# Weight conversions of the first layer in pinned slots, h·cos(h) read from PSUM, and w_in and w_out in tiles of their own

## The chip, the cores and the metric

The kernel runs on one core of one Trainium2 chip. The metric is the time of one launch in microseconds (us) of device time. Three runs of the kernel before gave 2143.59, 2143.5 and 2141.09 us, a median of 2143.5 us.

## The reference

Three layers follow one another, all in float32. Only the middle one and its inputs are touched by the change.

```python
attn_out = _attn_ref(q, k, v, w_phi)            # linear attention, 4 batches, 8 heads, 576 x 64
x = attn_out.transpose(0, 2, 1, 3).reshape(2304, 512)
h = x @ w_in                                    # 512 -> 2048
g = h * np.cos(h)
x = g @ w_out                                   # 2048 -> 512
P = sinkhorn(exp(x @ w_gate))                   # 8 rounds over 2304 x 8
out = sum_e P[:, e:e+1] * (np.maximum(x @ w1[e], 0) @ w2[e])    # 8 experts, 512 -> 1024 -> 512
```

w_in and w_out come as float64 and are used in float32.

## The kernel before, in words

Every float32 product is done as three passes: each operand is split into a high part (rounded to the matmul's format) and a low part (the remainder), and high·high, high·low and low·high are summed in PSUM (TensorE's output memory, eight banks).

**Conversion of the weights.** The chip reads the float64 words of w_in and w_out as pairs of 32-bit integers. Each of the 16 units of the middle layer (128 of its 2048 columns) has two halves, w_in and w_out, so there are 32 halves of 128x512 numbers; half h belongs to unit h // 2. A half goes through seven small steps (lines 125 to 162): `conv_fetch` loads the raw words (`raw`, two buffers), `conv_low` (ScalarE, output `csgn`), `conv_size` (VectorE, output `cmag`), `conv_floor` (VectorE, in the attention part GpSimd), `conv_high` (VectorE, a shift on `cmag` and then an operation with two inputs on `csgn`), `conv_join` (GpSimd, adds the two), `conv_round` (ScalarE, the high part in `csp`) and `conv_rest` (GpSimd, the low part; then a DMA stores both parts in the DRAM tile `wd`). The two parts are loaded back from `wd` whenever a unit is needed.

**Attention** (line 377) runs over 16 pairs of heads in a software pipeline with an order written out by hand (`ORDER`, line 534). While it runs, `pinned[0]` is true: every instruction that is issued through the wrappers `pe`, `ve`, `se` and `ge` (TensorE, VectorE, ScalarE, GpSimd; line 60) keeps its place in program order on its engine. Otherwise a planner orders the instructions of each engine by its own cost estimates. The DMAs on the SyncE queue (SP) are always placed by the planner, and each queue runs in order. Attention also converts halves 0 to 16, and half 17 up to `conv_join`.

**The middle layer** (`moe1_steps`, line 546) runs over blocks of tokens: blocks 0, 1 and 2 of 512 tokens each, then block 3 (512) together with block 4 (256). For each of the 16 units f it does `moe1_l1` (12 matmuls of 128x512 into one of two PSUM buffers `ph`, then the element-wise chain), and `moe1_l2` of unit f - 2 (12 matmuls that add into four PSUM banks `acc`). The generator stops after six matmuls of l1, at the end of l1, and twice in l2, so there are four steps per unit in the middle of a block and 64 in a block, and one more after it. After each step `tick()` issues work that was deferred, and for block 0 a piece of the conversion may follow.

The element-wise chain of a unit is: `y` (ScalarE, from `ph`), `h` (ScalarE, a copy of `ph`), `t` (ScalarE, rounds y), `y` (VectorE, t and y), then `second`: the sine (ScalarE) and h = sine times h (VectorE), and one step later `third`: `hh`, the high part (ScalarE), and `hl`, the low part (VectorE). A `ph` buffer is free again when `y` and `h` have been read out of it.

In block 0 the generator `convert` (line 356) is advanced on every second step, in three pieces per half: fetch, low, size, floor and high; join; round and rest. Where a unit is wanted before its halves are done, `next_unit` (line 540) advances `convert` until they are. `load_unit1` (line 96) loads both halves of a unit into one tile `wsp` (four buffers), in the program's order right before l1 of that unit.

After each block, `moe1_out` copies `acc` out, and `gate` (line 516) takes one `ph` buffer in the same rotation, between l1 of the next block's units 0 and 1, for the logits (`graw`, then `pick` and the copy into `logit`). The last layer follows; it does not change.

Of the kernel before, what the change touches and what calls it, by code (L numbers as in the profile page):

```python
# [9 lines left out]
F32 = mybir.dt.float32  # L10
F32R = mybir.dt.float32r
# [3 lines left out]
ALU = mybir.AluOpType  # L15
# [10 lines left out]
def kernel(ctx: ExitStack, tc: tile.TileContext, q, k, qk_rem, v, w_phi,  # L26
                         moe_w, moe2_w_gate, moe2_w1, moe2_w2, out):
    nc = tc.nc
    P = 128
    B, NP, _, MAIN = q.shape  # L30
    D = v.shape[-1]
    NTT, _, DM = out.shape
    NT = NTT * P
    NE, NQ = moe2_w1.shape[:2]
    KC = DM // P
    NF1 = moe_w.shape[0]
# [21 lines left out]
    pinned = [False]  # L58
# [16 lines left out]
    pe, ve, se, ge = Engine(nc.tensor), Engine(nc.vector), Engine(nc.scalar), Engine(nc.gpsimd)  # L75
# [17 lines left out]
    ps_h = ctx.enter_context(tc.tile_pool(name="ps_h", bufs=1, space=PSUM))  # L93
    wpool = mctx.enter_context(tc.tile_pool(name="wpool", bufs=4, side="right"))

    def load_unit1(f):
        w = wpool.tile([P, 2, 2, DM], F32R, name="wsp")
        for i in range(2):
            nc.sync.dma_start(out=w[:, i, :, :].bitcast(F32), in_=wd[f][:, i, :, :])
        return (tuple(w[:, 0, s, :].rearrange("p (k f) -> p k f", k=KC) for s in range(2)),  # L100
                tuple(w[:, 1, s, :] for s in range(2)))

    def mm3(ps, pairs):
        ops = []
# [17 lines left out]
    NHALF = 2 * NF1  # L122
    halves = {}

    def conv_fetch(h):
        raw = vpool.tile([P, DM, 2], I32, name="raw64")
        nc.sync.dma_start(out=raw.rearrange("p f t -> p (f t)"), in_=moe_w32[h // 2, h % 2])
        halves[h] = {"raw": raw}

    def conv_low(h):  # L130
        st = halves[h]
        st["sgn"] = vpool.tile([P, DM], I32, name="csgn")
        se.activation(out=st["sgn"].bitcast(F32), in_=st["raw"][:, :, 0].bitcast(U32), func=AF.Copy,
                      scale=2.0 ** -51, bias=2.0)

    def conv_size(h):
        st = halves[h]
        st["mag"] = vpool.tile([P, DM], I32, name="cmag", bufs=3)
        ve.tensor_scalar(out=st["mag"], in0=st["raw"][:, :, 1], scalar1=2 ** 31 - 1, scalar2=None, op0=ALU.bitwise_and)

    def conv_floor(h, eng):
        mag = halves[h]["mag"].bitcast(F32)
        eng.tensor_scalar(out=mag, in0=mag, scalar1=2.0 ** -15, scalar2=None, op0=ALU.max)

    def conv_high(h):
        st = halves[h]
        ve.tensor_scalar(out=st["mag"], in0=st["mag"], scalar1=3, scalar2=None, op0=ALU.logical_shift_left)
        ve.scalar_tensor_tensor(out=st["sgn"], in0=st["raw"][:, :, 1], scalar=-2 ** 31, in1=st["sgn"], op0=ALU.bitwise_and, op1=ALU.bitwise_or)

    def conv_join(h):  # L150
        st = halves[h]
        ge.tensor_tensor(out=st["mag"], in0=st["mag"], in1=st["sgn"], op=ALU.add)

    def conv_round(h):
        st = halves[h]
        st["sp"] = vpool.tile([P, 2, DM], F32R, name="csp")
        act_hi(st["sp"][:, 0, :], st["mag"].bitcast(F32))

    def conv_rest(h):
        st = halves.pop(h)  # L160
        pool_lo(st["sp"][:, 1, :], st["mag"].bitcast(F32), st["sp"][:, 0, :])
        nc.sync.dma_start(out=wd[h // 2][:, h % 2, :, :], in_=st["sp"].bitcast(F32))
# [191 lines left out]
            dve_lo(lo, raw, hi)  # L354

    def convert():
        h = B * NP + 1
        conv_round(h)
        yield
        conv_rest(h)  # L360
        done_conv[0] = (h + 1) // 2
        for h in range(h + 1, NHALF):
            if h + 1 < NHALF and h + 1 not in halves:
                conv_fetch(h + 1)
            conv_low(h)
            conv_size(h)
            conv_floor(h, ve)
            conv_high(h)
            yield
            conv_join(h)  # L370
            yield
            conv_round(h)
            conv_rest(h)
            done_conv[0] = (h + 1) // 2
            yield

    def attention():
        n = B * NP
        sts = {0: first}
        conv_fetch(0)  # L380
        conv_fetch(1)
        for i in range(n + 2):
            cur, prev, last = sts.get(i), sts.get(i - 1), sts.pop(i - 2, None)
            if i + 1 < n:
                sts[i + 1] = load_heads(*divmod(i + 1, NP))
            if cur is None and prev is not None:
                prev["pr_psum"] = {"small": ps_r.tile([P, MAIN], F32, name="sm")}
            small = cur or (prev or {}).get("pr_psum")
            for step in ORDER.split():
                if step in CONV:  # L390
                    h = i - (step in ("csp", "q"))
                    if 0 <= h < NHALF:
                        CONV[step](h)
                        if step == "c" and h + 2 < NHALF:
                            conv_fetch(h + 2)
                    continue
                if step == "KS" and cur and not prev:
                    load_values(cur)
                if step in STEP0:
                    if cur:  # L400
                        STEP0[step](cur)
                elif step in STEP1:
                    if prev:
                        STEP1[step](prev, small) if step == "Fr" else STEP1[step](prev)
                    if step == "KS" and cur:
                        load_values(cur)
                elif last:
                    {"X": lambda st: turn_x(st, small), "xh": x_high, "xl": x_low}[step](last)
# [16 lines left out]
    def moe1_l1(blk, unit, res):  # L425
        n = BW[blk]
        xh, xl = xblk[blk]
        wh, wl = unit[0]
        ph = hpsum()
        ops = []  # L430
        for c in range(KC):
            ops += [(wh[:, c, :], xh[:, c, :]), (wh[:, c, :], xl[:, c, :]), (wl[:, c, :], xh[:, c, :])]
        for i, (w, x) in enumerate(ops):
            pe.matmul(ph[:, 0:n], w, x, start=(i == 0), stop=(i == len(ops) - 1))
            if i == 5:
                yield 1.3
        h = mpool.tile([P, 512], F32, name="h", bufs=3)
        t = mpool.tile([P, 512], F32, name="t")
        y = mpool.tile([P, 512], F32, name="y")
        pool = hpool if n == MAIN else tpool[0]  # L440
        gh = pool.tile([P, n], F32R, name="hh")
        gl = pool.tile([P, n], F32R, name="hl")
        res += [gh, gl]
        se.activation(out=y[:, 0:n], in_=ph[:, 0:n], func=AF.Copy, scale=INV2PI, bias=0.25)
        se.copy(out=h[:, 0:n], in_=ph[:, 0:n])
        se.activation(out=t[:, 0:n], in_=y[:, 0:n], func=AF.Copy, bias=MAGIC)
        ve.scalar_tensor_tensor(out=y[:, 0:n], in0=t[:, 0:n], scalar=MAGIC, in1=y[:, 0:n],
                                       op0=ALU.subtract, op1=ALU.subtract)

        def second():  # L450
            se.activation(out=y[:, 0:n], in_=y[:, 0:n], func=AF.Sin, scale=-TWOPI)
            ve.tensor_tensor(out=h[:, 0:n], in0=y[:, 0:n], in1=h[:, 0:n], op=ALU.mult)

        def third():
            act_hi(gh, h[:, 0:n])
            dve_lo(gl, h[:, 0:n], gh)

        defer(MD, second)
        defer(2 * MD, third)
        yield 1.3  # L460
# [74 lines left out]
    MD = 1  # L535
    GD = 3

    units = []

    def next_unit():  # L540
        while done_conv[0] <= len(units) and done_conv[0] < NF1:
            next(conv, None)
        units.append(load_unit1(len(units) % NF1))
        return units[-1]

    def moe1_steps(*blks):
        pend = []
        for f in range(NF1 + LAG):
            if f < NF1:
                unit = next_unit()  # L550
                gs = []
                for blk in blks:
                    g = []
                    yield from moe1_l1(blk, unit, g)
                    gs.append(g)
                pend.append((f, unit, gs))
            if f >= LAG:
                f2, unit2, gs = pend.pop(0)
                for blk, g in reversed(list(zip(blks, gs))):
                    yield from moe1_l2(blk, f2, unit2, *g)  # L560
        for blk in reversed(blks):
            defer(1 if blk == B else GD, lambda blk=blk, x2=moe1_out(blk): gate(blk, *x2))
            yield 0.2
# [7 lines left out]

    pinned[0] = True
    attention()
    pinned[0] = False
    actx.close()
    hpool = mctx.enter_context(tc.tile_pool(name="hpool", bufs=4, side="right"))
    mpool = mctx.enter_context(tc.tile_pool(name="mpool", bufs=2, side="right"))
# [5 lines left out]
    for blk in range(B - 1):  # L583
        for i, _ in enumerate(moe1_steps(blk)):
            tick()
            if blk == 0 and i % 2:
                next(conv, None)
    ectx.close()

    xctx = ExitStack()  # L590
# [323 lines left out]
```

## Time and profile before

| | us |
|---|---|
| median of three runs | 2143.5 |
| the profiled execution's own time | 2141.93 |
| its span, first to last instruction | 2140.1 |
| TensorE busy in the span | 2089.5 |
| VectorE / GpSimd / ScalarE busy | 1274.5 / 1104.3 / 934.0 |

The profile's page gives the busy time of each engine, then the span in 40 slices of 53.5 us. TensorE's digits are these; slices 4 to 6 hold block 0 of the middle layer:

```profile
PE   8997989999999999999999999999999999999999
...
PEclk9999999999999999999999999999999999999999
```

A digit of 9 is a busy share of 90% or more; PEclk is the granted clock of TensorE in tenths of full speed. Busy time of TensorE counts pipelined matmuls, so the number of matmuls in a stretch says more than the share.

### The profile page before, as it was taken

What the parts mean: (1) busy time and instruction counts of PE and PEld (TensorE: products, weight loads), DVE (VectorE), ACT (ScalarE), POOL (GpSimd) and SP (SyncE); (2) the same over time, 40 slices, a digit from 0 to 9 for tenths busy, and PEclk for the clock granted to TensorE, in tenths of its full rate; (3) what the DMA queues carried; (4) which work ended last, traced back from release to release, by engine and by line L of the source; (5) the groups of instructions that cost most, each with busy time, mean ns of one, the idle gap of its engine ahead of it and who ended that gap; (6) DMA issues with size and microseconds to landing.
All of it is one profiled execution on the core that took longest, in us unless ns stands there. A gap on an engine that the chain in (4) does not pass through costs nothing.

```text
span 2140.1 us, 35117 instructions
## 1 busy us (share of the span) xinstructions
PE 2089.5 (98%) x14039; PEld 1846.2 (86%) x14039; DVE 1274.5 (60%) x2311; ACT 934.0 (44%) x1452; POOL 1104.3 (52%) x729
## 2 busy tenths in 40 slices
PE   8997989999999999999999999999999999999999
PEld 7896768878877898989999998989999998989998
DVE  6887643445448756665666655555555555555555
ACT  5675545556553334343433433343333334333431
POOL 3345310000036666765776676567667656766762
PEclk9999999999999999999999999999999999999999
DMA  7866765664330122222222211621111111111101
GB/s 237 254 181 203 279 218 196 203 231 141 125 117 30 49 80 67 90 78 67 83 74 84 62 49 50 219 70 40 50 40 50 47 43 50 40 50 40 50 30 45
DMA packets 97314, 220.01 MB, mean 103 GB/s; under 512 B 31872, under 2 KB 42368, under 8 KB 97152
## 3 DMA queue, kind: packets, MB, share of 16 engines
q1 hardware_dynamic: 97152, 217.78, 31.6%
q8 instruction: 110, 1.80, 0.4%
q14 instruction: 52, 0.43, 0.1%
HBM read 183.27 MB, written 34.47 MB: 102 GB/s over the span
## 4 chain that ended last, share of the span: by engine, by line
PE 89%; DVE 3%; issue 3%; POOL 2%; ACT 1%; DMA 1%; SPq 0%; POOLq 0%; DVEq 0%
PE py L68 36%; PE pm L68 32%; PE ph L68 8%; PE acc L68 7%; PE pk L68 2%; PE pp L68 1%; PE pn L68 1%; POOL cmag L68 1%; PE sm L68 1%; PE pu L68 1%; POOL csp L68 1%; PE px L68 0%; ACT csp L68 0%; DVE logit L818 0%; DVE r L748 0%
## 5 line engine op out<-in xcount | busy, mean ns | idle before, releaser
L794 DVE SCALAR_TENSOR_TENSOR acc<-py,logit,acc 128x512 f32<-128x512 f32 x531 | 396.6, 750 | 322.0 <-PE py L68 322.0
L68 PE MATMUL pm<-xch,w1h 128*128 128x288 f32 x1792 | 531.0, 296 | 2.8 <-DVE t L816 1.3
L68 PE MATMUL pm<-xch,w1l 128*128 128x288 f32 x1792 | 530.7, 297 | 0.0
L68 PE MATMUL pm<-xcl,w1h 128*128 128x288 f32 x1792 | 523.0, 292 | 0.0
L690 POOL TENSOR_TENSOR w1l<-raw,w1h 128x256 fp32r<-128x256 f32 x126 | 97.1, 792 | 759.9 <-ACT w1h L687 759.9
L68 PE MATMUL py<-w2h,hl 128*128 128x512 f32 x1152 | 451.6, 392 | 3.8 <-POOL hl L68 3.8
L68 PE MATMUL py<-w2l,hh 128*128 128x512 f32 x1152 | 451.2, 392 | 0.0
L68 PE MATMUL py<-w2h,hh 128*128 128x512 f32 x1152 | 450.4, 391 | 0.8 <-DVE acc L794 0.8
L68 POOL TENSOR_TENSOR hl<-r,hh 128x1152 fp32r<-128x1152 f32 x128 | 344.7, 2693 | 78.7 <-ACT hh L68 72.9
L68 PEld LDWEIGHTS pm<-xcl,w1h 128*128 128x128 f32 x1792 | 341.1, 190 | 5.2 <-issue 0.4
L68 PEld LDWEIGHTS pm<-xch,w1h 128*128 128x128 f32 x1792 | 336.6, 188 | 9.4 <-DVE t L816 1.6
L68 PEld LDWEIGHTS pm<-xch,w1l 128*128 128x128 f32 x1792 | 336.2, 188 | 0.0
L768 ACT ACTIVATE r<-r 128x1152 f32<-128x1152 f32 x128 | 149.1, 1165 | 268.5 <-DVE r L748 262.2
L68 PEld LDWEIGHTS py<-w2h,hl 128*128 128x128 f32 x1152 | 216.5, 188 | 50.3 <-POOL hl L68 4.6
L68 PEld LDWEIGHTS py<-w2h,hh 128*128 128x128 f32 x1152 | 216.7, 188 | 44.8 <-DVE acc L794 2.8
L68 PEld LDWEIGHTS py<-w2l,hh 128*128 128x128 f32 x1152 | 216.8, 188 | 42.5
L744 ACT COPY keep<-pm 128x288 f32<-128x288 f32 x256 | 102.0, 399 | 343.6 <-PE pm L68 343.5
L748 DVE TENSOR_TENSOR r<-r,pm 128x288 f32<-128x288 f32 x512 | 216.0, 453 | 41.5 <-PE pm L68 41.3
L690 POOL TENSOR_TENSOR w1l<-ssum,w1h 128x1280 fp32r<-128x1280 f32 x63 | 186.7, 2964 | 2.0 <-ACT w1h L687 0.3
L68 PE MATMUL ph<-xh,wsp 128*128 128x512 f32 x512 | 174.7, 403 | 11.0 <-DMA wsp<-wd 5.8
L748 DVE TENSOR_TENSOR r<-keep,pm 128x288 f32<-128x288 f32 x128 | 58.2, 455 | 208.1 <-PE pm L68 207.6
L68 PE MATMUL acc<-hh,wsp 128*128 128x512 f32 x512 | 169.6, 396 | 10.3 <-ACT hh L68 10.3
(143 smaller groups left out, 2849.6 us busy)
## 6 DMA issues: line engine op xcount, KB each, us to landing
raw<-in_moe_w_dram SPq DMA_DIRECT2D x160, 512.0 KB, 3.5
wsp<-wd SPq DMA_DIRECT2D x128, 512.0 KB, 4.8
wd<-csp SPq DMA_DIRECT2D x32, 512.0 KB, 3.3
xcd<-xs SPq DMA_DIRECT2D x14, 576.0 KB, 5.1
out_dram<-acc SPq DMA_DIRECT2D x18, 256.0 KB, 2.3
vx<-in_v_dram SPq DMA_DIRECT2D x17, 256.0 KB, 4.6
Tk<-in_k_dram SPq DMA_DIRECT2D x16, 256.0 KB, 4.9
Tq<-in_q_dram SPq DMA_DIRECT2D x16, 256.0 KB, 5.1
```

The costliest lines, as they stand in the source:

```text
L68: ins = call(*args, **kwargs)
L690: eng.tensor_tensor(out=lo[:, sl], in0=src, in1=hi[:, sl].bitcast(F32), op=ALU.subtract)
L744: nc.scalar.copy(out=t, in_=ps[m])
L748: nc.vector.tensor_tensor(out=r[:, u, th, :], in0=r[:, u, th, :] if a is None else ps[a], in1=ps[b], op=op)
L768: nc.scalar.activation(out=rf, in_=rf, func=AF.Relu)
L794: nc.vector.scalar_tensor_tensor(out=a, in0=py, scalar=pe, in1=a, op0=ALU.mult, op1=ALU.add)
```

## The change

Four edits. The loads of w_in and w_out get tiles of their own (`wi`, `wo`, four buffers each, together as large as `wsp` was); w_in is asked for two units ahead, w_out with its own unit. The copy of `ph` into `h` goes, and the product h·cos(h) reads `ph` itself. `convert` now starts with half 17, which attention leaves out, and is advanced on every step of block 0, again in three pieces per half (here A, B and C): A is low and size of half h and after them rest of half h - 1 with its store; B is floor, high, the fetch of half h + 1 if it is still to be done, and join; C is round. And `pinned[0]` stays true through block 0, so that the planner no longer orders these engines there. `done_conv` counts halves where it counted units.

```diff
--- before.py
+++ after.py
@@ -93,12 +93,11 @@
     ps_h = ctx.enter_context(tc.tile_pool(name="ps_h", bufs=1, space=PSUM))
     wpool = mctx.enter_context(tc.tile_pool(name="wpool", bufs=4, side="right"))
 
-    def load_unit1(f):
-        w = wpool.tile([P, 2, 2, DM], F32R, name="wsp")
-        for i in range(2):
-            nc.sync.dma_start(out=w[:, i, :, :].bitcast(F32), in_=wd[f][:, i, :, :])
-        return (tuple(w[:, 0, s, :].rearrange("p (k f) -> p k f", k=KC) for s in range(2)),
-                tuple(w[:, 1, s, :] for s in range(2)))
+    def load_half1(f, i):
+        w = wpool.tile([P, 2, DM], F32R, name=f"w{'io'[i]}")
+        nc.sync.dma_start(out=w.bitcast(F32), in_=wd[f][:, i, :, :])
+        parts = [w[:, s, :] for s in range(2)]
+        return [x.rearrange("p (k f) -> p k f", k=KC) for x in parts] if i == 0 else parts
 
     def mm3(ps, pairs):
         ops = []
@@ -354,25 +353,26 @@
             dve_lo(lo, raw, hi)
 
     def convert():
-        h = B * NP + 1
-        conv_round(h)
-        yield
-        conv_rest(h)
-        done_conv[0] = (h + 1) // 2
-        for h in range(h + 1, NHALF):
-            if h + 1 < NHALF and h + 1 not in halves:
-                conv_fetch(h + 1)
-            conv_low(h)
-            conv_size(h)
-            conv_floor(h, ve)
-            conv_high(h)
+        first = B * NP + 1
+        for h in range(first, NHALF + 1):
+            if h < NHALF:
+                if h not in halves:
+                    conv_fetch(h)
+                conv_low(h)
+                conv_size(h)
+            if h > first:
+                conv_rest(h - 1)
+                done_conv[0] = h
             yield
-            conv_join(h)
-            yield
-            conv_round(h)
-            conv_rest(h)
-            done_conv[0] = (h + 1) // 2
-            yield
+            if h < NHALF:
+                conv_floor(h, ve)
+                conv_high(h)
+                if h + 1 < NHALF and h + 1 not in halves:
+                    conv_fetch(h + 1)
+                conv_join(h)
+                yield
+                conv_round(h)
+                yield
 
     def attention():
         n = B * NP
@@ -389,6 +389,8 @@
             for step in ORDER.split():
                 if step in CONV:
                     h = i - (step in ("csp", "q"))
+                    if h > n:
+                        continue
                     if 0 <= h < NHALF:
                         CONV[step](h)
                         if step == "c" and h + 2 < NHALF:
@@ -442,14 +444,13 @@
         gl = pool.tile([P, n], F32R, name="hl")
         res += [gh, gl]
         se.activation(out=y[:, 0:n], in_=ph[:, 0:n], func=AF.Copy, scale=INV2PI, bias=0.25)
-        se.copy(out=h[:, 0:n], in_=ph[:, 0:n])
         se.activation(out=t[:, 0:n], in_=y[:, 0:n], func=AF.Copy, bias=MAGIC)
         ve.scalar_tensor_tensor(out=y[:, 0:n], in0=t[:, 0:n], scalar=MAGIC, in1=y[:, 0:n],
                                        op0=ALU.subtract, op1=ALU.subtract)
 
         def second():
             se.activation(out=y[:, 0:n], in_=y[:, 0:n], func=AF.Sin, scale=-TWOPI)
-            ve.tensor_tensor(out=h[:, 0:n], in0=y[:, 0:n], in1=h[:, 0:n], op=ALU.mult)
+            ve.tensor_tensor(out=h[:, 0:n], in0=y[:, 0:n], in1=ph[:, 0:n], op=ALU.mult)
 
         def third():
             act_hi(gh, h[:, 0:n])
@@ -535,19 +536,24 @@
     MD = 1
     GD = 3
 
-    units = []
-
-    def next_unit():
-        while done_conv[0] <= len(units) and done_conv[0] < NF1:
-            next(conv, None)
-        units.append(load_unit1(len(units) % NF1))
-        return units[-1]
+    units = [[], []]
+    NU = NF1 * B
+
+    def weights1(i, g):
+        while len(units[i]) <= min(g, NU - 1):
+            n = len(units[i])
+            while done_conv[0] <= 2 * n + i and n < NF1:
+                next(conv)
+            units[i].append(load_half1(n % NF1, i))
 
     def moe1_steps(*blks):
         pend = []
         for f in range(NF1 + LAG):
             if f < NF1:
-                unit = next_unit()
+                g0 = blks[0] * NF1 + f
+                weights1(0, g0 + 2)
+                weights1(1, g0)
+                unit = units[0][g0], units[1][g0]
                 gs = []
                 for blk in blks:
                     g = []
@@ -571,7 +577,7 @@
 
     pinned[0] = True
     attention()
-    pinned[0] = False
+    done_conv[0] = B * NP + 1
     actx.close()
     hpool = mctx.enter_context(tc.tile_pool(name="hpool", bufs=4, side="right"))
     mpool = mctx.enter_context(tc.tile_pool(name="mpool", bufs=2, side="right"))
@@ -583,8 +589,9 @@
     for blk in range(B - 1):
         for i, _ in enumerate(moe1_steps(blk)):
             tick()
-            if blk == 0 and i % 2:
+            if blk == 0:
                 next(conv, None)
+        pinned[0] = False
     ectx.close()
 
     xctx = ExitStack()
```

## Rows read from the trace of the kernel before

**Rows 1.** Windows: block 0, a stretch of block 1, five slow microseconds. Columns named in line one.

```profile
core 0: us, PE busy (x) PEld busy (x) DVE busy (x) ACT busy (x) POOL busy (x), PEclk, DMA share, GB/s
171.90:298.20 126.30, 104.69 (x398) 80.38 (x396) 75.76 (x110) 63.91 (x114) 47.44 (x36) 0.89 0.73 253
322.00:375.00 53.00, 53.00 (x235) 43.89 (x234) 20.06 (x30) 27.94 (x49) 0.00 (x0) 1.00 0.57 194
260.00:265.00 5.00, 5.00 (x12) 3.94 (x13) 4.97 (x8) 1.07 (x2) 2.64 (x2) 0.50 0.90 302
```

**Rows 2.** Waits of TensorE, 161 to 330 us: total us, times, longest us.

```profile
PE acc L68 <- ACT hh L68: 10.3, 3, 6.0
PE ph L68 <- DMA wsp<-wd: 5.8, 2, 2.9
PE ph L68 <- ACT h L68: 2.7, 2, 2.5
PE ph L68 <- DVE xl L68: 2.2, 1, 2.2
```

**Rows 3.** Timeline, one unit's element-wise chain, block 1: start, duration, engine, operation [idle before].

```profile
392.81 0.60 ACT L68 ACTIVATE y<-ph 128x512 f32<-128x512 f32 x1
...
393.31 0.58 ACT L68 COPY h<-ph 128x512 f32<-128x512 f32 x1
...
393.77 0.64 ACT L68 ACTIVATE t<-y 128x512 f32<-128x512 f32 x1
...
394.45 0.69 DVE L68 SCALAR_TENSOR_TENSOR y<-t,y 128x512 f32<-128x512 f32 x1 [0.94 <-ACT t L68]
...
395.18 0.63 ACT L68 ACTIVATE y<-y 128x512 f32<-128x512 f32 x1 [0.76 <-DVE y L68]
...
395.84 0.69 DVE L68 TENSOR_TENSOR h<-y,h 128x512 f32<-128x512 f32 x1 [0.70 <-ACT y L68]
...
396.66 0.63 ACT L68 CAST hh<-h 128x512 fp32r<-128x512 f32 x1
...
397.32 0.69 DVE L68 TENSOR_TENSOR hl<-h,hh 128x512 fp32r<-128x512 f32 x1 [0.79 <-ACT hh L68]
```

**Rows 4.** Timeline of VectorE, GpSimd and ScalarE, one half's conversion in block 0.

```profile
230.16 0.89 DVE L68 TENSOR_SCALAR cmag<-cmag 128x512 f32<-128x512 f32 x2
...
231.56 0.68 DVE L68 SCALAR_TENSOR_TENSOR csgn<-raw,csgn 128x512 int32<-128x512 int32 x1
...
232.33 1.29 POOL L68 TENSOR_TENSOR cmag<-cmag,csgn 128x512 int32<-128x512 int32 x1 [6.18 <-DVE csgn L68]
...
233.65 0.62 ACT L68 CAST csp<-cmag 128x512 fp32r<-128x512 f32 x1 [1.33 <-POOL cmag L68]
...
234.35 1.30 POOL L68 TENSOR_TENSOR csp<-cmag,csp 128x512 fp32r<-128x512 f32 x1 [0.73 <-ACT csp L68]
```

**Rows 5.** Timeline: VectorE operations that meet a GpSimd operation.

```profile
161.41 1.27 POOL L68 TENSOR_TENSOR cmag<-cmag,csgn 128x512 int32<-128x512 int32 x1 [2.89 <-DVE csgn L68]
...
162.38 0.68 DVE L68 TENSOR_TENSOR xl<-px,xh 128x512 fp32r<-128x512 f32 x1
...
232.35 1.81 DVE L68 TENSOR_TENSOR h<-y,h 128x512 f32<-128x512 f32 x1
...
234.85 1.34 DVE L68 TENSOR_TENSOR hl<-h,hh 128x512 fp32r<-128x512 f32 x1 [0.69 <-ACT hh L68]
```

**Rows 6.** Timeline of ScalarE at the start of block 0.

```profile
173.87 0.68 ACT L68 ACTIVATE csgn<-raw 128x512 f32<-128x512 uint32 x1 [3.35 <-DMA raw<-in_moe_w_dram]
...
186.15 1.28 ACT L68 ACT_TABLE_LOAD   x1
```

**Rows 7.** DMA issues, 165 to 285 us: KB each, median us to landing.

```profile
raw<-in_moe_w_dram SPq DMA_DIRECT2D x15, 512.0 KB, 5.1
```

**Rows 8.** Timeline of TensorE, from block 0 to block 1.

```profile
298.23 1.06 PE L68 MATMUL ph<-x2f,graw 128*32 128x512 f32 x8
...
299.46 0.50 PE L68 MATMUL ph<-xh,wsp 128*128 128x512 f32 x1 [0.17 <-ACT h L68]
...
300.95 0.95 PE L68 MATMUL ph<-pick,lt 128*128 128x8 f32 x8
```

## The prediction, on record before the run

> **What bounds the kernel now.** I read the page's slices first: TensorE is near full everywhere except at the start, in slices 4 to 6 (block 0 of the middle layer) and around 640 us. Then windows, for matmuls per microsecond. In block 1 it is 235 in 53 us, 0.2255 us each, so a group of 12 takes 2.71 us and a unit (24) 5.41 us; block 0 takes 126.3 us from its first matmul to the gate behind it [rows 1]. In it lie 384 matmuls of its own and the 12 of block 1's first l1: 396 x 0.2255 = 89.3 us. So block 0 loses 37 us, and that is all the change can win there. TensorE's waits name 21 us of it: 10.3 for `hh`, 5.8 for weights on their way back from DRAM, 2.7 for the copy that frees `ph`, 2.2 for attention's last `xl` [rows 2]. Much of the rest is the clock: in the five microseconds behind one of these waits it is granted 0.50 (1.2 of 2.4 GHz) and 12 matmuls pass where 22 would [rows 1]. Blocks 1 to 4 run without such gaps; nothing is to be won there.
>
> **The start.** Attention's last `xh` stood behind a conversion step that waited 3.35 us for its raw words [rows 6]. With half 17 left to block 0 and the order pinned, that step comes later, so l1 of unit 0 runs through: 171.9 + 2.71 = 174.6. Then y 0.60, t 0.64, a load of the sine's table 1.28, sine 0.63, product 0.69, with 0.04 between them: the first product ends at 178.6 [rows 1, 3, 6]. Unit 2 needs that `ph` buffer and starts there.
>
> **Separate tiles and loads.** Same bytes, same memory; SP issues as many DMAs as before. Counting steps: before unit f the generator has been advanced 4f - 4 times, half h is stored at advance 3(h - 17) + 4, and unit f asks for half 2f + 4. That holds for every f, with at least a half to spare, and nothing is forced any more. So I take the 5.8 us of weight waits out, and the forced conversions at the block's end with them.
>
> **The pinned slots.** These decide. TensorE needs 5.41 us per unit and a slot is a quarter of it. But ScalarE, VectorE and GpSimd now each run in program order, and the question is how long their own loop takes. Per unit: y, t, (VectorE) y, sine, product, then hh, hl [rows 3]. Per half: low 0.68, size about 0.43, floor and shift 0.89 together, the two-input step 0.68, join 1.29, round 0.62, low part 1.30 [rows 4, 6]. ScalarE starts its next operation 0.5 us after a 0.6 us one, VectorE 0.6 after a 0.69 one [rows 3]. Three units hold 12 slots, so four halves, after which the pattern repeats.
>
> One more thing governs it: a VectorE operation with both inputs in SBUF doesn't run beside a GpSimd one. The product that began with a join (232.35 beside 232.33) took 1.81 us instead of 0.69, ending 0.54 after it; hl at 234.85 took 1.34 beside the low part. `xl`, which reads PSUM, took 0.68 beside a join [rows 4, 5]. So the new product is free of this, and the others aren't.
>
> Now by hand, in us from the end of a join. First unit (slots A, B, C, A): round 0.7, low, y 1.75, t 2.4, VectorE's y 3.15, sine 3.8, product 4.55, then B's three VectorE steps to 5.9; hl slips in ahead of the join, which ends at 7.7. Second unit (B, C, A, B): round 8.4, low, y 9.5, t 10.15; VectorE does size and floor, is held by the low part until 9.7, B ends at 10.6, y 11.2, sine 11.9, product 12.6 (the join runs beside it), round 13.05, hh 13.6, hl held to 14.95, A and B to 16.8, join 18.1. Third (C, A, B, C): round 18.75, y 19.3, t 19.95, VectorE's y held to 20.65, sine 21.3, product 22.05, hh 22.7, hl 23.4, B 24.8, join 26.1.
>
> So three units take 26.1 us, 8.7 each against TensorE's 5.41: pinned this way, moe chain and conversion chain hardly overlap, and TensorE waits for `ph` about 3 us in every unit. Its being ahead by two buffers doesn't help, since the loop never waits for TensorE. If nothing were held between VectorE and GpSimd, the same list gives 23.7 us. From the first product at 178.6, halves 17 to 28 and nine units are three periods, and the product of unit 12, behind the last half, comes at 178.6 + 78.3 + 22.05 = 279. TensorE then has l1 of units 14 and 15, l2 of 12 to 15 and block 1's first l1: 7 x 2.71 = 19.0, to 298.0, and half a slow-clock group, 1.2 (bounds 0 and 2.7) [rows 1]: 299.2. Before, the gate began at 298.23 [rows 8]. So block 0 comes out even: **+1 us**.
>
> Behind SP: the fetch of half h + 1 can go out only after B of half h - 1 has freed its buffer, and in a queue that also holds the store of h - 1, which waits for the low part. It lands 5.1 us after its issue [rows 7]. Issued early it is in time; issued where the program has it (6.0 in the list) it lands at 11.1, 2.8 late for A at 8.3. Over three periods 0 to 9 us; I take **1.5**, near the low end, since mostly its store, not its place in the program, will hold it.
>
> **h·cos(h) from PSUM.** The copy (0.58) goes 80 times from ScalarE, which bounds nothing in blocks 1 to 4: 0. The product itself: 0.69 from SBUF, 0.68 for `xl` from PSUM [rows 3, 5]: 0. The Trainium skill (VectorE: DVE Perf Modes, § The TRN2 errata) gives VectorE a fixed 120 cycles from PSUM against 58 from SBUF, an estimate of 0.065 us per product, some 0.8 us over the 13 in the loop, and the sum would be 2153; no such difference shows in these two rows.
>
> What it costs: `ph` is held until the product, not the copy. Chain without the copy: 0.60 + 0.64 + 0.69 + 0.63 + 0.69 and handoffs = 3.4 us behind l1. Inside a block the same buffer is wanted 3 x 2.71 = 8.1 us later: free. At a block's start the gate takes the other buffer, so l1 of unit 1 wants unit 0's back at once. Before it began at 299.46, 1.23 after the gate's start [rows 8]; now 3.4 after l1's end (298.2), 301.6, less the 0.95 of `pick` that fills part: 2.1 - 0.95, and about 0.5 because VectorE has the logits' copy in the way: **1.65 us** (bounds 1.2 and 2.7). This comes twice, and from block 2 to 3, where three more buffers are wanted in a row and VectorE is busy with the last layer's inputs, I put **2.5** (bounds 1.6 and 4). Together +5.8 (4.0 to 9.4).
>
> **Sum.** 1.0 + 1.5 + 5.8 = +8.3 us on the profiled execution's own 2141.9 (span 2140.1): 2150. The runs' median, 2143.5, lies 1.6 above it, and against it I predict 2143.5 + 8.3 = **2152 us**.
>
> **Rivals.**
> - *The conversions disappear beside the matmuls.* If ScalarE and VectorE kept up, block 0 from 178.6 is 31 groups x 2.71 = 84.0: gate at 262.6, 35.6 earlier; less 5.8, 2114 us. Partly, between 2114 and 2137. For it: VectorE is busy only 76 of 126 us in block 0 [rows 1]. Against it: VectorE's own work and its wait for the sine alone come to about 6 us per unit in the new order.
> - *GpSimd holds VectorE little.* Period 23.7: the twelfth product at 178.6 + 71.1 + 19.9 = 269.6, the gate at 289.8; -8.4 + 5.8 = -2.6: 2141 us, no change. For it: orders in which a GpSimd operation meets the PSUM product. Against it: [rows 5].
> - *Raw words come late.* All 9 us of the fetch, and the starts of blocks at their upper bound: 8.3 + 7.5 + 3.6 = +19.4, 2163 us. It decides once the fetch stands behind its place in the program on SP. For it: a 5.1 us landing against a 6.5 us half.
>
> **How the numbers follow.** Forecast 0.52, hidden 0.18, little holding 0.20, late data 0.10. A difference of 0.2% (4.3 us) is about what a measurement of this kernel can tell from none. Faster: the hidden case and 0.04 of little holding, 0.22. Same: 0.16 of that and 0.08 of the forecast's lower edge, 0.24. Slower: 0.54. The forecast's own range is 2146 to 2158. For 8 in 10 I go down into half of the hidden case, 2128, and up to the late one, 2164.
>
> **What would show it.** Right: in block 0 `ph` matmuls wait for VectorE's h, about 3 us per unit, units follow at 8 to 9 us until the last half, and no matmul waits for `wi` or `wo`; l1 of unit 1 in each later block waits 1 to 3 us for h. Wrong: units at 5.4 to 6 us with conversions running, which gives the hidden case; csgn waiting for raw in most halves, the late one; products beside joins longer than 0.7 us, a fault in what I made of PSUM.

## The result, and the profile after

Four runs of the changed kernel gave 2152.37 to 2156.43 us, a median of **2154.8 us**; four runs of the kernel before on the same chip had a median of 2142.3 (2140.25 to 2143.59). The ratio is 1.0061, with a 95% interval of 1.0048 to 1.0075: slower by 12.5 us. The forecast was 2152, with +8.3. The profiled execution took 2154.34 us, its span is 2152.6, against 2141.93 and 2140.1 before.

On the page of the changed kernel block 0 is weak again, in slices 4 to 6 (8, 7, 8; before 7, 9, 8), and TensorE's granted clock in slice 5 is 8 tenths, before 9:

```profile
PE   8998789999998999999999999999999999999999
...
PEclk9999899999999999999999999999999999999999
```

A loss of 12.5 us in 2150 is not to be seen at that scale, so I compared landmarks in TensorE's timelines: the last transposes of attention (`px`), the first matmul of each of the three gates (`graw`), and the last layer's first matmul (`pm`). From the one to the next, in us:

| stretch | before | after | difference |
|---|---|---|---|
| attention's end to gate 1 (block 0) | 127.2 | 131.5 | +4.3 |
| gate 1 to gate 2 (block 1) | 89.40 | 92.13 | +2.7 |
| gate 2 to gate 3 (block 2) | 90.18 | 92.13 | +1.95 |
| gate 3 to `pm` (blocks 3 and 4) | 136.1 | 141.0 | +4.9 |

Attention itself ended 1.4 us earlier, so gate 1 comes 2.9 us later (301.14; before 298.23 [rows 8]). Behind `pm` nothing differs. So 2.9 us of the 12.5 come from block 0 and 9.6 from the three later starts of blocks.

**Block 0.** One window of the changed kernel, all of block 0 from attention's last `px` (columns as in [rows 1]).

```profile
169.62:301.14 131.52, 105.14 (x404) 81.64 (x404) 70.80 (x113) 58.88 (x99) 46.57 (x35) 0.91 0.75 252
```

That is 404 matmuls; the kernel before has 405 between the same two marks, in 127.2 us. No engine but TensorE is busy for much over half of the time. Waits of TensorE, 165 to 340 us (total, times, longest):

```profile
PE ph L68 <- DVE h L68: 25.2, 12, 3.7
...
PE ph L68 <- DVE xl L68: 1.1, 1, 1.1
```

The waits for weights, for `hh` and for the copy [rows 2] are gone; one wait has taken their place, for the product that frees `ph`. TensorE's timeline shows that it comes with a beat:

```profile
201.53 0.50 PE L68 MATMUL ph<-xh,wi 128*128 128x512 f32 x1 [3.09 <-DVE h L68]
210.27 0.50 PE L68 MATMUL ph<-xh,wi 128*128 128x512 f32 x1 [1.40 <-DVE h L68]
218.31 0.50 PE L68 MATMUL ph<-xh,wi 128*128 128x512 f32 x1 [2.31 <-DVE h L68]
227.81 0.50 PE L68 MATMUL ph<-xh,wi 128*128 128x512 f32 x1 [2.14 <-DVE h L68]
...
254.05 0.80 PE L68 MATMUL ph<-xh,wi 128*128 128x512 f32 x1 [3.71 <-DVE h L68]
...
280.30 0.62 PE L68 MATMUL ph<-xh,wi 128*128 128x512 f32 x1 [3.71 <-DVE h L68]
```

From 201.53 to 227.81 it is 26.28 us for three units; the list worked out by hand had 26.1. The last such release, behind the last half, is at 280.30; forecast was 279.

Why the loop is long shows in the timeline of ScalarE, VectorE and GpSimd:

```profile
201.51 0.62 ACT L68 CAST hh<-h 128x512 fp32r<-128x512 f32 x1 [0.20 <-DVE h L68]
...
204.34 1.39 POOL L68 TENSOR_TENSOR cmag<-cmag,csgn 128x512 int32<-128x512 int32 x1 [4.79 <-DVE csgn L68]
...
205.76 0.62 ACT L68 CAST csp<-cmag 128x512 fp32r<-128x512 f32 x1 [3.63 <-POOL cmag L68]
206.29 0.67 ACT L68 ACTIVATE csgn<-raw 128x512 f32<-128x512 uint32 x1
...
206.87 0.58 ACT L68 ACTIVATE y<-ph 128x512 f32<-128x512 f32 x1
...
209.53 0.69 DVE L68 TENSOR_TENSOR h<-y,ph 128x512 f32<-128x512 f32 x1 [0.69 <-ACT y L68]
```

ScalarE is through with `hh` at 202.13, then idles 3.63 us, since next in its order stands the round of a half whose join ends at 205.7. Behind it stands `y` of a unit whose l1 was complete before 201.53, where TensorE began the next one. That unit's product comes at 209.53 and releases TensorE at 210.27. In block 0 `csp` waits 41.2 us for the join in this way.

**Starts of blocks.** TensorE's and VectorE's timeline of the changed kernel behind gate 1 and behind gate 3:

```profile
301.14 1.06 PE L68 MATMUL ph<-x2f,graw 128*32 128x512 f32 x8
303.10 1.06 PE L68 MATMUL ph<-pick,lt 128*128 128x8 f32 x8 [0.89 <-DVE lt L68]
304.34 0.69 DVE L68 TENSOR_TENSOR h<-y,ph 128x512 f32<-128x512 f32 x1
304.44 0.79 PE L68 MATMUL ph<-xh,wi 128*128 128x512 f32 x1 [0.28 <-DVE logit L68]
...
485.40 1.14 PE L68 MATMUL ph<-x2f,graw 128*32 128x512 f32 x8
489.05 1.88 PE L68 MATMUL ph<-pick,lt 128*128 128x8 f32 x8 [2.51 <-DVE lt L68]
491.21 0.80 PE L68 MATMUL ph<-xh,wi 128*128 128x512 f32 x1 [0.28 <-DVE logit L68]
```

Since the product holds unit 0's buffer, the planner has put `pick` ahead of l1 of unit 1. That l1 begins at 304.44, while unit 0's product still reads its buffer (304.34 to 305.03), and behind the copy of the logits; so it is in the gate's buffer. It starts 3.30 us after the gate, where it was 1.23 before [rows 8]. And the clock falls. Windows of four microseconds behind gate 1, of the changed kernel and then of the one before:

```profile
301.14:305.14 4.00, 2.83 (x19) 1.73 (x19) 2.12 (x4) 1.93 (x4) 0.00 (x0) 0.91 0.86 295
305.14:309.14 4.00, 4.00 (x14) 3.18 (x13) 0.69 (x1) 0.54 (x1) 0.00 (x0) 0.66 0.09 38
309.14:313.14 4.00, 4.00 (x19) 3.33 (x18) 0.73 (x2) 2.53 (x5) 0.00 (x0) 1.00 0.37 122
```

```profile
298.23:302.23 4.00, 3.83 (x25) 2.62 (x25) 1.57 (x4) 2.23 (x4) 0.00 (x0) 1.00 1.08 263
302.23:306.23 4.00, 4.00 (x20) 3.30 (x19) 1.89 (x3) 2.68 (x5) 0.00 (x0) 1.00 0.44 170
306.23:310.23 4.00, 4.00 (x19) 3.31 (x18) 2.30 (x4) 2.83 (x6) 0.00 (x0) 1.00 0.08 19
```

Six matmuls are missing in the first window, mainly by the stall, and six in the second, where the clock is granted at 0.66, between its levels of 1.2 and 2.4 GHz; in the third all is as before. Twelve matmuls of 0.2255 us are 2.7 us, what gate 2 is late by.

What the wait costs without the clock shows in the experiment with the rounds put later (below). At its gate 1, at 295.60, TensorE makes the same two waits, of 0.89 and 0.28, but its clock stays full. First a line of its timeline, then the second window of four microseconds:

```profile
297.56 1.06 PE L68 MATMUL ph<-pick,lt 128*128 128x8 f32 x8 [0.89 <-DVE lt L68]
```

```profile
299.60:303.60 4.00, 4.00 (x20) 3.26 (x19) 0.69 (x1) 0.81 (x2) 0.00 (x0) 1.00 0.51 180
```

Its gates 1 and 2 are 90.59 us apart, against 89.40 before and 92.13 in the changed kernel. So the wait costs 1.2 us, and the clock, where it falls, 1.5 more. At gate 2 of the same run the waits are the same and the clock falls to 0.59: 92.16. Why it falls at one and not at the other stays open.

### The profile page after: what moved, and what is told of

It is laid out like the page before. It is cut to its first block, busy times and chain, and to the rows that moved or that the text cites. A ratio compares the mean times of both kernels' runs of the same rounds, so it can differ in the third digit from the quotient of the medians.

```text
span 2152.6 us, 35111 instructions
## 1 busy us (share of the span) xinstructions
PE 2095.8 (97%) x14039; PEld 1853.4 (86%) x14039; DVE 1268.8 (59%) x2312; ACT 909.5 (42%) x1372; POOL 1103.2 (51%) x728
## 4 chain that ended last, share of the span: by engine, by line
PE 89%; DVE 3%; issue 3%; POOL 3%; DMA 1%; ACT 1%; SPq 0%; POOLq 0%; DVEq 0%
PE py L68 36%; PE pm L68 32%; PE ph L68 8%; PE acc L68 7%; PE pk L68 2%; PE pp L68 1%; PE pn L68 1%; POOL cmag L68 1%; POOL csp L68 1%; PE sm L68 1%; PE pu L68 1%; DMA raw<-in_moe_w_dram 0%; ACT csp L68 0%; PE px L68 0%; DVE logit L825 0%
## 5 line engine op out<-in xcount | busy, mean ns | idle before, releaser
L68 PE MATMUL ph<-xh,wi 128*128 128x512 f32 x512 | 180.4, 415 | 27.2 <-DVE h L68 25.2
L68 PE MATMUL acc<-hh,wo 128*128 128x512 f32 x512 | 167.8, 390 | 0.0
```

Of the source, the lines that this page charges most:

```text
L68: ins = call(*args, **kwargs)
```

## The experiments

Theory: two things cost time, the pinned order in block 0 (a loop of three engines that wait for one another) and the product from PSUM at the starts of blocks. Rivals: the loop is bound by VectorE's meetings with GpSimd and PSUM, not by the order; raw words that come late; the separate tiles. Each edit is against the changed kernel, except that of the separate tiles, which is against the kernel before. Times are medians; the kernel before had 2142.2, 2142.1 and 2141.6 in the three batches. "Block 0" is from attention's last `px` to gate 1, 131.5 us in the changed kernel.

### One part undone at a time

**The order.** Only the pin is lifted:

```diff
     attention()
+    pinned[0] = False
     done_conv[0] = B * NP + 1
```

> The changed kernel with the pin taken off again in block 0; the slots, the separate tiles and the product from PSUM stay. Theory (the order in which ScalarE, VectorE and GpSimd take the two chains sets block 0's pace): the planner moves conversion steps off the element-wise chain where it can, units of block 0 come closer together than 8.8 us and the gate behind block 0 comes some 5 to 15 us before 301.1, so 2140 to 2150 us against 2154.8 for the changed kernel; a planner that keeps to program order would give no difference. Rival (the pace is that of the conversion work itself, whatever its order: raw words, or GpSimd and VectorE holding each other): within 3 us of 2154.8, gate at 298 to 304 us.

Measured: 2137.67 us, ratio 0.9985 (0.9976 to 0.9994), 17 us under the changed kernel. Block 0 is 113.1 us, 18.4 shorter; the gates stay 92.2 apart. Waits in block 0, without the pin:

```profile
ACT csp L68 <- POOL cmag L68: 26.3, 13, 3.2
...
PE ph L68 <- DVE h L68: 12.9, 6, 5.7
...
DVE y L68 <- ACT t L68: 7.9, 4, 5.4
```

In the changed kernel these were 41.2, 25.2 and 35.0. With the same operations and the same slots, the planner's order lets `y` and `t` go past the rounds. So the order is the loop's price, more of it than I had expected.

**The copy of `ph`.** It comes back in all blocks:

```diff
+        se.copy(out=h[:, 0:n], in_=ph[:, 0:n])
...
-            ve.tensor_tensor(out=h[:, 0:n], in0=y[:, 0:n], in1=ph[:, 0:n], op=ALU.mult)
+            ve.tensor_tensor(out=h[:, 0:n], in0=y[:, 0:n], in1=h[:, 0:n], op=ALU.mult)
```

> The changed kernel with ScalarE's copy of ph back in all blocks, the product reading the copy; slots, pin and tiles stay. Theory (holding ph until the product costs at every block's start, and inside block 0 TensorE only waits for a loop on the other engines): the waits at the starts of blocks 1 to 3 go, 9.6 us less behind the first gate (gates 89 to 90.5 us apart instead of 92.1); in block 0 the loop of three units gets longer than 26.3 us, by three times 0.3 us for the copy in front of t and up to 1.2 us where a product meets a join, so 27 to 28.5 us, and TensorE waits for hh instead of ph: gate 3 to 9 us later than 301.1. Sum 2148 to 2154 us. Rival (ph being held is what slows block 0): units of block 0 below 8 us, the gate 10 us or more before 301, 2135 us or less.

Measured: 2145.75 us, ratio 1.0022 (1.0012 to 1.0031). Gate 2 comes 89.4 us after gate 1, as before the change. The loop is longer, as expected (releases at 198.95, 225.89 and 252.81, so 26.9 us), but block 0 is 131.1 us and not longer: a miss in that part. Three periods lose 2.0 us in this way. But the first of these releases comes 29.6 us after attention's end, and 31.9 in the changed kernel, since the copy frees `ph` ahead of the product; that makes up for it. From the last release, at 279.75, to the gate both take the same, 20.7 and 20.8 us. VectorE's product in block 0, by form, from the copy and then from PSUM in the changed kernel:

```profile
L68 DVE TENSOR_TENSOR h<-y,h 128x512 f32<-128x512 f32 x16 | 12.5, 783 | 11.4 <-ACT y L68 11.4
```

```profile
L68 DVE TENSOR_TENSOR h<-y,ph 128x512 f32<-128x512 f32 x16 | 11.0, 688 | 11.1 <-ACT y L68 11.1
```

**The same from block 1 on only**, so that block 0 keeps the product from PSUM:

```diff
+        if blk:
+            se.copy(out=h[:, 0:n], in_=ph[:, 0:n])
...
+            ve.tensor_tensor(out=h[:, 0:n], in0=y[:, 0:n], in1=(h if blk else ph)[:, 0:n], op=ALU.mult)
```

> The changed kernel with ScalarE's copy of ph back in blocks 1 to 4 alone; block 0 as changed. Theory: block 0 is as in the changed kernel (gate at 301 us, give or take 1), the block starts are as before the change (gates 89.4 and 90.2 us apart, 136.1 us from the third to the last layer's first matmul): 9.6 us less, 2145 us, 2 to 3 us above the kernel before. Rival (the 9.6 us behind the first gate come from the separate loads of w_in and w_out or from another order by the planner): no more than 3 us less, 2152 us.

Measured: 2146.41 us, ratio 1.0025 (1.0014 to 1.0035). TensorE's timeline behind gate 1:

```profile
302.99 1.07 PE L68 MATMUL ph<-x2f,graw 128*32 128x512 f32 x8
304.23 0.50 PE L68 MATMUL ph<-xh,wi 128*128 128x512 f32 x1 [0.17 <-ACT h L68]
...
305.72 0.95 PE L68 MATMUL ph<-pick,lt 128*128 128x8 f32 x8
```

l1 is back at 1.24 us after the gate, ahead of `pick`. Gates 1, 2 and 3 are 89.4 us apart. So 8.4 us of the 12.5 are the product from PSUM in blocks 1 to 4, and it is their starts that change.

**The order by hand, otherwise.** Still pinned, but the round of half h - 1 stands in slot C behind the join of half h, so its input is long there, and the rest of h - 2 in A:

```diff
-            if h > first:
-                conv_rest(h - 1)
+            if h > first + 1:
+                conv_rest(h - 2)
...
                 conv_join(h)
-                yield
-                conv_round(h)
-                yield
+            yield
+            if first < h <= NHALF:
+                conv_round(h - 1)
+            yield
```

> The changed kernel with the rounding of a half moved one half later (piece C rounds half h - 1 beside half h, its low part and store another half later); the same instructions, the same pin, the product from PSUM. Theory (in program order ScalarE waits for the join, and y and t of the next unit wait behind it: 41 us of such waits): the loop of three units falls from 26.3 us to about 20.4 by the same hand count, units at 6.8 us, the gate some 20 us before 301.1, 2130 to 2139 us. Rival (the pace is the sum of work on VectorE and GpSimd, which hold each other): three units stay above 24 us, less than 8 us gained. Rival (raw words come too late): the loop doesn't shorten and csgn waits for raw.

Measured: 2145.01 us, ratio 1.0018 (1.001 to 1.0027): a gain of 9.8 where 20 were expected, and outside the expected 2130 to 2139. The profiled execution, the slowest of eleven, gained 6.8, and its block 0 is 124.3 us, 7.3 shorter. Its waits name what is late now:

```profile
ACT csgn L68 <- DMA raw<-in_moe_w_dram: 18.4, 8, 5.3
...
PE ph L68 <- DMA wi<-wd: 7.4, 2, 3.9
```

In the changed kernel no `csgn` waited for raw words. The rival of late words holds as soon as the loop is shorter.

**The words earlier**, on top of the last: a third buffer, and the fetch of half h + 2 in slot B.

```diff
-        raw = vpool.tile([P, DM, 2], I32, name="raw64")
+        raw = vpool.tile([P, DM, 2], I32, name="raw64", bufs=3)
...
-                if h + 1 < NHALF and h + 1 not in halves:
-                    conv_fetch(h + 1)
+                if h + 2 < NHALF:
+                    conv_fetch(h + 2)
```

> The run with the rounding a half later, with a third buffer for the raw words and each fetch issued a half earlier. Theory: the loop is short of raw words now (ScalarE waited 18.4 us for them in block 0), so with them in time three units fall to some 20 to 21 us and block 0, from attention's last transposes to the gate, from 124 us to 112 to 118: 2133 to 2139 us. Rival (VectorE and GpSimd holding each other set the pace by now): the waits for raw go and y and the join wait longer instead, less than 3 us gained, 2142 us or more.

Measured: 2132.58 us, ratio 0.9955 (0.994 to 0.997), a little under the expected range. Block 0 is 109.8 us, 14.5 shorter than without the early words, and `csgn` waits 1.0 us in all. The loop shows in ScalarE's timeline, four halves from the one to the other:

```profile
197.40 0.67 ACT L68 ACTIVATE csgn<-raw 128x512 f32<-128x512 uint32 x1
...
217.60 0.68 ACT L68 ACTIVATE csgn<-raw 128x512 f32<-128x512 uint32 x1
```

20.20 us instead of 26.28 (in the changed kernel the same two stand at 206.29 and 232.56), with the same operations, pin and product. Later periods take up to 21.5. So it is not pinning as such that costs, but where in the order a wait stands.

**Separate tiles alone**, put into the kernel before, which keeps its conversions on every second step, its copy and its planner:

```diff
+    def load_half1(f, i):
+        w = wpool.tile([P, 2, DM], F32R, name=f"w{'io'[i]}")
...
+                weights1(0, g0 + 2)
+                weights1(1, g0)
```

> The kernel before with one edit of the change alone: w_in and w_out in tiles of their own, w_in asked for two units ahead; conversions, their pace on every second step and the copy of ph as before. Theory: the two waits for weights (5.8 us) go, but with w_in asked for two units ahead the conversions are forced from unit 10 on instead of 12, as crowded as before, so hh is still late behind them: 2135 to 2143 us, no more than 7 us gained. Rival (the loads were the whole loss): 15 us or more gained, 2127 us.

Measured: 2137.36 us, ratio 0.9981 (0.9972 to 0.999). Some 4 us are won, in block 0 (122.9 from 127.2). The time is in the expected range, but not for the expected reason. TensorE's waits:

```profile
PE ph L68 <- DMA wi<-wd: 7.8, 3, 4.1
PE acc L68 <- ACT hh L68: 5.3, 1, 5.3
```

The waits for weights were to go and are longer instead, 7.8 us where they were 5.8 [rows 2]; what is shorter is the wait for `hh` (10.3 before). That the changed kernel has no wait for weights is thus not the tiles' doing alone; that its halves are converted in time is the likely rest, not shown by a run of its own.

### Parts together, and the end of it

**No late conversion at all:** halves 17 to 31 are not converted, their units load other units' weights.

```diff
     def convert():
-        first = B * NP + 1
...
+        done_conv[0] = NHALF
+        yield
```

> The changed kernel without the conversion of halves 17 to 31: the loads of these halves take halves already converted in their place (unit f - 8), all else as changed, the pin and the product from PSUM too. Theory (the conversions in the pinned order are what stretches block 0): units at 5.41 us, block 0 from attention's last transposes to the gate 91 to 95 us instead of 131.5, 2115 to 2119 us. Rival (holding ph, or the pin by itself, slows block 0): units above 6 us, 2125 us or more.

Measured: 2115.96 us, ratio 0.9878 (0.9865 to 0.9892), block 0 95.0 us. So converting costs the changed kernel 38.8 us, 36.5 of them in block 0, and the case of hidden conversions was worked out to the right size (2114).

**Pin lifted and the copy from block 1 on:** the edits of the first and third experiment together.

> The run without the pin, with ScalarE's copy of ph back in blocks 1 to 4. Theory (pin in block 0 and held ph at the block starts are two separate costs): block 0 stays at 113 us from attention's last transposes to the gate, and the 8.4 us that the copy gave in the pinned kernel come off again: 2137.7 - 8.4 = 2129 us, 13 us under the kernel before. Rival (with the planner free, the starts of the blocks were filled already): 2135 to 2138 us.

Measured: 2129.99 us, ratio 0.9945 (0.9933 to 0.9958). The two costs add up.

**The same with the early words:**

> The run without the pin and with the copy in blocks 1 to 4, and also a third buffer for the raw words with each fetch a half earlier. Theory: the unpinned block 0 waits for raw words too (ScalarE 12.9 us, VectorE 9.8), but only where TensorE has slack for part of it: 2 to 8 us less than without the third buffer, 2121 to 2127 us. Rival (the transfers share one bandwidth and come no earlier): same within 2 us, about 2129 us.

Measured: 2126.98 us, ratio 0.9932 (0.992 to 0.9945). Its interval meets that of the one before, so the 3 us are likely, not shown. In the profiled executions block 0 is 8.0 us shorter with the early words (105.0 against 113.0), but attention's last `px` comes 6.9 us later (178.07 against 171.18): without the pin more conversion steps stand ahead of `xn` on VectorE, and TensorE waits 8.55 us for it. So most of the 8.0 us is work moved ahead and not time won.

**The late rounds, early words, pinned, and the copy from block 1 on:**

> Pinned, rounding a half later, third buffer for raw words, and ScalarE's copy of ph back in blocks 1 to 4. Theory: the block starts give the same 8.4 us here: 2132.6 - 8.4 = 2124 us, some 3 us under the unpinned run with the same buffers (2127.0), which would make this the fastest of all. Rival (the third buffer shifted the starts of the blocks too): 2130 us or more.

Measured: **2125.56 us, ratio 0.9923 (0.991 to 0.9937)**, the fastest of all: 29 us under the changed kernel and 16 under the one before (2141.6 in this batch). Its block 0 is 110.6 us; what is left there above the 95.0 is partly TensorE's waits for `wi` (7.0 us) and for `h` (4.8).

## Why the prediction was right, step by step

The pin and the product from PSUM have prices from runs that differ in one edit each; the rest has one price together. The separate tiles, the slots on every step with half 17 in them, and the product from PSUM in block 0 alone, all without the pin, bring 2142 to 2130.0 (-12); the pin adds 16.4 (2146.4); the product from PSUM in blocks 1 to 4 adds 8.4 (2154.8). The forecast of +8.3 lies 4.2 us under the measured +12.5 and names the same two causes; of these 4.2 us, 3.8 are in the starts of blocks.

- **The start:** the first product began at 179.42 and ended at 180.1, not 178.6. l1 of unit 0 did not run through: attention ended 1.4 us earlier, but TensorE waited 1.14 us for its last `xl`, so l1 began at 171.65, near the 171.9 of the forecast. What was left out is the clock behind this wait: the first seven matmuls took 3.1 us and not 1.6. The two lines are VectorE's and TensorE's in the changed kernel:

```profile
179.42 0.69 DVE L68 TENSOR_TENSOR h<-y,ph 128x512 f32<-128x512 f32 x1 [0.70 <-ACT y L68]
...
180.17 0.50 PE L68 MATMUL ph<-xh,wi 128*128 128x512 f32 x1 [1.35 <-DVE h L68]
```

- **Weight waits removed:** right, no matmul waits for `wi` or `wo` [rows 2]. What they were worth alone no run shows: the tiles by themselves won some 4 us, with weights still waited for.
- **The pinned loop:** 26.28 us against 26.1 by hand, last release at 280.30 against 279, from the first release (180.17) to the last 100.1 against 279 - 178.6 = 100.4. This step carried the forecast. The loop by hand gave every engine its real order; the shares of busy time gave no hint of it.
- **Raw words late, +1.5:** nothing in this kernel; the store and fetch were early enough. That it made up for the late start, so that gate 1 at 301.14 stands beside a forecast of 300.7, is chance. The 26 us loop hid it, and the experiment that shortened the loop met it at once (18.4 us of waits).
- **The copy from ScalarE, 0, and the product from PSUM, 0:** right as to the operation: 688 ns on average, at most as long as from SBUF [rows 3]. The rule of the Trainium skill that was weighed (VectorE: DVE Perf Modes, § The TRN2 errata), of a longer fixed time from PSUM, doesn't agree with this number: by an estimate from its table it would be 65 ns more than from SBUF.
- **The starts of blocks, +5.8: the term that was mis-sized.** It measured 9.6, just above its own bound of 9.4. The buffer was held as forecast, but the sign that was named, l1 of unit 1 waiting 1 to 3 us for `h`, did not come: the planner avoided that wait by `pick`, and what TensorE waits for is `lt` (0.89) and the copy of the logits (0.28). The price of the wait was about right, 1.2 us against 1.65. Left out was TensorE's clock, which is full there before the change and falls behind the wait after it: another 1.5 us each at the first two starts. That block 2 is late by 1.95 and not by 2.7 is a gain elsewhere: late in block 2 the kernel before waits 0.49 us for `hl` (at 472.37), the changed one doesn't. From block 2 to 3, 4.9 came instead of 2.5: `lt` is 2.51 us late, where VectorE has the last layer's inputs to prepare, and the clock is 0.50 for the four microseconds behind:

```profile
485.40:489.40 4.00, 1.49 (x11) 0.58 (x10) 3.89 (x7) 2.66 (x5) 0.00 (x0) 0.92 0.78 248
489.40:493.40 4.00, 3.72 (x13) 3.23 (x13) 2.61 (x6) 1.52 (x3) 0.00 (x0) 0.50 0.45 100
```

I had the clock in front of me in block 0, where [rows 1] shows 0.50 behind a wait, and priced it at that block's end, but neither at its start nor where the change makes a new wait.

- **The rivals.** Hidden conversions: false, the beat is 8.8 us per unit and not 5.4. GpSimd holding VectorE little: false in this kernel, for the holds are in the trace (below), but how much of the loop they make was not measured in a run of its own. Raw late: false here, true of a faster order.

The rival theory of the experiments, that the loop is bound by what VectorE does, falls for the loop of 26.28 us: with late rounds and early words the same VectorE work ran in 20.20. In that faster loop VectorE is busy for 17.2 us of them, so there its meetings with GpSimd may set the pace; no run tested it.

## What to carry to other kernels

Before an order across several engines is pinned, write out one period of it by hand, engine by engine, and look for an operation that waits with ready work behind it; here one round, put a half later, was worth 6 us in every 26 once the raw words came early too. When a copy out of PSUM is dropped, the buffer is held for the whole chain behind it: look at the places where the buffers' rotation changes, not at the steady state. And behind a wait that a change makes on TensorE the clock may fall: here the same wait cost 1.2 us where the clock stayed full and 2.7 where it fell.

## What the runs showed of the hardware

VectorE and GpSimd held one another in both directions, and one operation with a single input, the size step, was held too. VectorE's and GpSimd's timeline of the changed kernel:

```profile
211.53 0.68 DVE L68 TENSOR_TENSOR hl<-h,hh 128x512 fp32r<-128x512 f32 x1
211.69 1.67 POOL L68 TENSOR_TENSOR cmag<-cmag,csgn 128x512 int32<-128x512 int32 x1 [3.94 <-DVE csgn L68]
212.13 1.51 DVE L68 TENSOR_SCALAR cmag<-raw 128x512 int32<-128x512 int32 x1
...
216.35 1.65 POOL L68 TENSOR_TENSOR cmag<-cmag,csgn 128x512 int32<-128x512 int32 x1 [0.96 <-DVE csgn L68]
...
217.56 0.69 DVE L68 TENSOR_TENSOR h<-y,ph 128x512 f32<-128x512 f32 x1 [0.70 <-ACT y L68]
...
219.20 1.37 DVE L68 TENSOR_TENSOR hl<-h,hh 128x512 fp32r<-128x512 f32 x1 [0.95 <-ACT hh L68]
...
220.49 0.42 DVE L68 TENSOR_SCALAR cmag<-raw 128x512 int32<-128x512 int32 x1
```

A join that begins within an `hl` takes 1.67 us instead of 1.29 [rows 4]. The size step takes 0.42 alone and 1.51 beside that join, ending 0.28 after it. The product that reads PSUM takes 0.69 while a join runs. The Trainium skill (SBUF — State Buffer, § SBUF: two separate sides) has the pair of ports that the two engines share as an exclusive lock: a GpSimd operation, or a VectorE one that has two SBUF inputs or runs in a two-port mode, holds it for the whole instruction if it starts first. The rows agree. That a VectorE operation with one SBUF input is among those that are held, the rows show for this size step; in which mode VectorE ran it, they don't.
